# One load per attention tile, issued behind its buffer's last reader, and a third first-layer group queued ahead of step 0

## The chip, the cores and the metric

One core of a Trainium2 chip runs the kernel. The metric is the device time of one execution in microseconds (us), shown as the median of three runs. The engines are named as in the profile: PE (TensorE), PEld (its weight loads), DVE (VectorE), ACT (ScalarE), POOL (GpSimd) and SP (SyncE, which only issues DMAs).

## What is computed

The reference chains three parts over 3072 tokens (4 batches of 768) of width 384 (8 heads of 48):

```python
for t in range(S):                       # linear attention with decay w and bonus u
    cur = np.einsum('bhd,bhe->bhde', u[None] * kt, vt)
    y[:, :, t] = np.einsum('bhd,bhde->bhe', rt, state + cur)
    state = wt[..., None] * state + np.einsum('bhd,bhe->bhde', kt, vt)
h = x @ w_in                             # dense layer, 384 -> 2048 -> 384
x = (np.maximum(h, 0) + alpha * np.minimum(h, 0)) @ w_out
logits = xn @ en.T / tau                 # 8 experts, top 1 by cosine
out[mask] = gate_w[mask, None] * (np.maximum(x[mask] @ w1[e], 0) @ w2[e])
```

## The kernel before, in words

The tokens are cut into 24 tiles of 128 (tile n) and 8 blocks of three tiles (block j). The attention is done chunk by chunk, a tile at a time. Its work is split into ten pieces a0 to a9 (`ATT`, L393): a0 and a1 are decay scans on DVE (L261, L270), a2 and a3 transposes and scores on PE, a4 (`att_p4`) the outputs on PE (L362, L365), a5 the transposition of the result for the dense layer, a8 (`att_w`, L274) a check of the decays on ACT.

A tile's inputs come as one DMA of 1.35 MB on SP's queue (`load_att`, L157, issued at L165; two DMAs for tiles 0 to 5). The pool `ld` has two buffers, so the load of tile n+2 overwrites tile n (tile 2 has a place of its own) and waits for every reader of tile n, of which a4 is the last. `run` (L860) calls `load_att(n + 2)` behind each of the pieces 4, 8 and 9 of a tile n above 2. In the main loop pieces 4 and 8 occur, piece 9 doesn't.

The dense layer runs in steps T (loop at L950), 16 to a block. A step runs one group of the first layer (`l1`, 9 matmuls into `h_ps`, L407; ACT L411 and DVE L412 make `m`, ACT L421 and DVE L426 split it into `gh` and `gl`) and, two steps behind, one of the second layer (`l2`, 9 matmuls into three `o_ps`, L436). In the program's text a step is: split of block 0's `m`, pieces a2 to a5, l1, l2, pieces a0, a1, a6 and a8, and then `step`, which advances the routing. Pieces lie on steps by a table: tile n begins at step t0, piece a8 stands at t0+3, a4 at t0+6, and for a block j of 3 or more the three tiles have t0 = 16(j-1) + {-4, 1, 7} (`AT`, L81).

At the end of block j's second layer, at T = 16j+17, `o_evac` (L440) copies the three `o_ps` into `rows` (ACT L446, DVE L444). There are three `o_ps` buffers and one `rows` buffer. The routing (`route`, L452) works on `rows` a piece a step and stores its three parts to DRAM (`x2d`, L520, on SP's queue) at T = 16j+29, 16j+30 and 16j+31. The next `o_evac`, at T = 16j+33, needs these stores to be done.

Ahead of step 0 a list (`PLAN`, L78) orders the first attention pieces ("a2.1" is piece 2 of tile 1), the conversion of the dense weights ("c2.1": stage 2 of chunk 1; four stages L196, L198/L199, L210, L212 on ACT and DVE), the first groups of layer 1 ("l1.0") and matmuls that only keep PE busy ("w4": four of L391, which write the same two `ps_h` buffers as `h_ps`). The weights come in 16 chunks through four `stg` buffers (L185, L187, on SP's queue); a chunk's load is issued when the chunk four before it has been converted, in steps 0 to 10 two steps ahead of its use. In steps 32 to 55 SP also stores 24 tiles of zeros to `out` (L982), one a step. Later, experts are gathered and run (L689 to L796); the change doesn't touch that.

Of the kernel before, what the change touches and what calls it, by code (L numbers as in the profile page):

```python
# [22 lines left out]
NTILE = B * NCH  # L23
# [51 lines left out]
LAGS = [0, 1, 4, 4, 6, 7, 2]  # L75

LOADS = [(0, "w"), (0, "rk"), "id", "v", (0, "n"), "e", (1, "w"), (1, "rk"), (1, "n"), (2, "w"), (2, "rk"), (2, "n"), 0, 1, 2, 3, "u"]
PLAN = "a0.0 a1.0 a8.0 a2.0 w6 a6.0 a3.0 a7.0 w8 a0.1 a1.1 a6.1 s a4.0 a3.1 a9.0 a2.1 e c0.0 a7.1 a9.1 w8 a0.2 c0.1 c0.2 a1.2 a6.2 c1.0 a4.1 w8 a3.2 c1.1 a7.2 a5.0 a5.1 c2.0 w4 a4.2 p0.0 c3.0 a5.2 c2.1 c1.2 l1.0 c3.1 c2.2 l1.1 p1.0 c0.3 c3.2 w4 a8.1 a2.2 a9.2"  # L78

AT1 = [0, 4, 8]  # L80
AT = {2: [-1, 6], 3: [-4, 1, 7]}  # L81
# [12 lines left out]
def tile_main(ctx, tc, keep, x2d, tbl, att, w_in, w_out, alpha, u_row, u_col, emb, tau, w1, w2, cst, out):  # L94
# [62 lines left out]
    def load_att(n, part=None):  # L157
        if n not in ld_t:
            if n == 2:
                ld_t[n] = att2[:, 0:LD]  # L160
            else:
                ld_t[n] = ldp.tile([128, LD], F32, tag="ld", name="ld")
        m = LN + 2 * DM if n in ND else LN
        for s in {None: [slice(0, LN), slice(m, LD)] if n in ND else [slice(0, LD)], "w": [slice(LD - LW, LD)], "rk": [slice(0, LN)], "n": [slice(m, LD - LW)]}[part]:
            SP.dma_start(out=ld_t[n][:, s], in_=att[n][:, s])  # L165
# [15 lines left out]
    def load_stage(kind, g):  # L181
        t = sgp.tile([128, GF * DM, 2], I32, tag="sg", name="stg")
        if kind == "in":
            for k in range(KD):
                SP.dma_start(out=t[:, k * GF * 128:(k + 1) * GF * 128, :], in_=w_in[:, k, 2 * g * GF * 128:2 * (g + 1) * GF * 128])  # L185
        else:
            SP.dma_start(out=t, in_=w_out[:, g * GF:(g + 1) * GF, :])  # L187
        stage[kind, g] = t

    def conv(q, kind, g):  # L190

        t = stage[kind, g]
        lw, hw = t[:, :, 0], t[:, :, 1]
        lf = lw.bitcast(F32)
        if q == 0:
            ACT.activation(out=lf, in_=lw.bitcast(U32), func=AF.Copy, scale=-0.936 * 2.0 ** -51, bias=-2.0)  # L196
        elif q == 1:
            DVE.scalar_tensor_tensor(out=lw, in0=hw, scalar=3, in1=lw, op0=ALU.logical_shift_left, op1=ALU.bitwise_or)  # L198
            DVE.scalar_tensor_tensor(out=lw, in0=hw, scalar=0x3FFFFFFF, in1=lw, op0=ALU.bitwise_or, op1=ALU.bitwise_and)  # L199
        else:  # L200
            h, g0 = divmod(g, NG // 2)
            if kind == "in":
                hi, lo = (w[:, :, g0 * GW:(g0 + 1) * GW] for w in win[h])
            else:
                if h == len(wout):
                    wout_half()
                hi, lo = (w[:, g0 * GF:(g0 + 1) * GF, 0:DM] for w in wout[h])
            f3 = lf.rearrange("p (a b) -> p a b", a=(KD if kind == "in" else GF))
            if q == 2:
                ACT.activation(out=hi, in_=f3, func=AF.Copy, scale=-1.0)  # L210
            else:
                DVE.scalar_tensor_tensor(out=lo, in0=f3, scalar=-1.0, in1=hi.bitcast(F32), op0=ALU.mult, op1=ALU.subtract)  # L212
                del stage[kind, g]
# [173 lines left out]
    def warm(n):  # L387

        for _ in range(n):
            t = ps_h.tile([128, 3, 128], F32, tag="h", name="idle")  # L390
            PE.matmul(out=t, lhsT=oneb, rhs=oneb.rearrange("p (o t) -> p o t", o=1).to_broadcast([128, 3, 128]), start=True, stop=True)  # L391
# [4 lines left out]
    g_t, m_t, o_t = {}, {}, {}  # L396
# [20 lines left out]
    def l1_hi(j, f):  # L417
        nt = BLK[j] * CH
        gh = gp.tile([128, nt], F32R, tag="gh", name="gh")
        gl = gp.tile([128, nt], F32R, tag="gl", name="gl")  # L420
        ACT.activation(out=gh, in_=m_t[j, f], func=AF.Copy)  # L421
        g_t[j, f] = (gh, gl)

    def l1_lo(j, f):
        gh, gl = g_t[j, f]
        DVE.tensor_tensor(out=gl, in0=m_t.pop((j, f)), in1=gh.bitcast(F32), op=ALU.subtract)  # L426
# [376 lines left out]
    if True:  # L803
# [54 lines left out]
        ran = set()  # L858

        def run(kind, *a):  # L860
            if (kind, *a) in ran:
                return
            if kind != "w":
                ran.add((kind, *a))
            if kind == "a":
                q, n = a
                ATT[q](n)
                m = n + 3 if n < 2 else n + 2
                if q in (4, 8, 9) and n != 2 and m < NTILE and (n > 2 or {("a", i, n) for i in (4, 8, 9)} <= ran):
                    load_att(m)  # L870
            elif kind == "c":
                q, c = a
                conv(q, ("in", "out")[c % 2], c // 2)
                if q == 3 and c + NSG < 2 * NG:
                    load_stage(("in", "out")[(c + NSG) % 2], (c + NSG) // 2)
            elif kind == "w":
                warm(*a)
            elif kind == "l":
                (l1, l2)[a[0] - 1](0, a[1])
            elif kind == "p":  # L880
                (wprime_a, wprime_b)[a[0]](a[1])
            elif kind == "e":
                ep = ps_a.tile([128, KD, NE], F32, tag="a", name="ep")
                for k in range(KD):
                    PE.transpose(ep[:, k, :], en[:, k * 128:(k + 1) * 128], ident[0:NE, 0:NE])
                ACT.activation(out=enT, in_=ep, func=AF.Copy)
            else:
                DVE.tensor_scalar(out=en2, in0=en2, scalar1=1e-6, scalar2=None, op0=ALU.add)
                DVE.reciprocal(out=en2, in_=en2)
                ACT.activation(out=en, in_=en, func=AF.Copy, scale=en2)  # L890

        def pieces(T, qs):
            for q, n in sched.get(T, []):
                if q in qs:
                    run("a", q, n)
                    if q == 6:
                        run("a", 7, n)

        def convs(T, late):
            for q, i in CONV[late]:  # L900
                c = T + OFF - i
                if 0 <= c < 2 * NG:
                    run("c", q, c)
# [20 lines left out]
        def early_loads():  # L924
            for s in range(ES):
                ids_load(s)
                if s == 0:
                    pump()
                    yield
            for s in range(ES):  # L930
                for t in range(2):
                    gather(s, t)
                yield
# [13 lines left out]

        for t in PLAN.split():
            run(t[0], *(int(i) for i in t[1:].split(".") if i))
        for T in range(16 * NB + 2):  # L950
            j, f = divmod(T, 16)
            for k in sorted(k for k in m_t if k[0] == 0 and k[1] <= T):
                l1_hi(*k)
                l1_lo(*k)
            pieces(T, (2, 3, 4, 5))
            convs(T, 0)
            if j < NB:
                run('l', 1, f) if j == 0 else l1(j, f)
            for i, d in enumerate(WPD):
                c = T + OFF - d  # L960
                if c % 2 and 0 <= c < 2 * NG:
                    run("p", i, c // 2)
            if T == 16 * (NB - 1):
                xg.extend(atp.tile([128, 2, ROW], F32, tag=t, name="xg") for t in ("st", "st", "at"))
                for t in xg:
                    POOL.memset(t, 0.0)
            if T >= 2:
                run('l', 2, T - 2) if T < 18 else l2((T - 2) // 16, (T - 2) % 16)
                if (T - 2) % 16 == 15:
                    o_evac((T - 2) // 16)  # L970
                    q = (T - 2) // 16
                    bg.append(chain(route(q), *((early_table(), early_loads()) if q == NB - 2 else (last_table(),) if q == NB - 1 else ())))
            convs(T, 1)
            pieces(T, (0, 1, 6, 8))
            if j and (j, f) in m_t:
                l1_lo(j, f)
            step(STEP7 if j >= NB - 1 else 1)
            if T == 32:
                zero = sgp.tile([128, DM], F32, tag="sg", name="zero")
                POOL.memset(zero, 0.0)  # L980
            if 32 <= T < 32 + NTILE:
                SP.dma_start(out=out[(T - 32) * CH:(T - 31) * CH, :], in_=zero)  # L982
            for fn, i, at in EARLY:
                if T - 16 * NB == at:
                    (split, x_T)[fn](0, i)
# [31 lines left out]
        n = len(STEPS)  # L1017
# [318 lines left out]
```

## Time and profile before

| | us |
|---|---|
| median of 3 runs (lowest, highest) | 885.43 (881.11, 886.57) |
| the profiled execution | 884.76 |
| its span in the trace | 882.9 |
| PE busy, share of the span | 811.0, 92% |
| DVE, ACT, POOL busy | 582.1, 433.2, 299.7 |

The span is the traced part of the profiled execution; the execution's own time lies 1.9 us above it. A duration below is from that execution. "Idle before" of a row is the time in which its engine waited ahead of it, and the name behind it is what ended the wait. PEclk is the TensorE clock that was granted, 1.00 for 2.4 GHz and 0.50 for 1.2 GHz.

### The profile page before, as it was taken

What the parts mean: (1) busy time and instruction counts of PE and PEld (TensorE: products, weight loads), DVE (VectorE), ACT (ScalarE), POOL (GpSimd) and SP (SyncE); (2) the same over time, 40 slices, a digit from 0 to 9 for tenths busy, and PEclk for the clock granted to TensorE, in tenths of its full rate; (3) what the DMA queues carried; (4) which work ended last, traced back from release to release, by engine and by line L of the source; (5) the groups of instructions that cost most, each with busy time, mean ns of one, the idle gap of its engine ahead of it and who ended that gap; (6) DMA issues with size and microseconds to landing.
All of it is one profiled execution on the core that took longest, in us unless ns stands there. A gap on an engine that the chain in (4) does not pass through costs nothing. (4 is left out here: it accounts for less than half of the span.)

```text
span 882.9 us, 16507 instructions
## 1 busy us (share of the span) xinstructions
PE 811.0 (92%) x6466; PEld 768.6 (87%) x6466; DVE 582.1 (66%) x1229; ACT 433.2 (49%) x861; POOL 299.7 (34%) x365
## 2 busy tenths in 40 slices
PE   9798899995996999699799879999899999999996
PEld 5598799895996899699699879999789999999996
DVE  7798867764671676468358367372897776767672
ACT  6776544442342434234333343432555676767672
POOL 2012122241232222123212321214446777676641
PEclk9999999996999799799889989999999999999999
DMA  9636532456349255333503630006567778686850
GB/s 318 203 109 234 198 127 69 184 100 216 103 164 193 88 162 144 135 127 75 204 12 124 161 111 1 28 28 233 170 126 253 228 263 281 212 285 208 289 179 31
DMA packets 34504, 140.71 MB, mean 159 GB/s; under 512 B 6076, under 2 KB 13468, under 8 KB 29808
## 3 DMA queue, kind: packets, MB, share of 16 engines
q1 hardware_dynamic: 20464, 79.70, 29.1%
q0 software_dynamic: 13952, 59.86, 20.8%
q8 instruction: 53, 0.87, 0.4%
q14 instruction: 35, 0.29, 0.1%
HBM read 125.20 MB, written 15.51 MB: 159 GB/s over the span
## 5 line engine op out<-in xcount | busy, mean ns | idle before, releaser
L412 DVE TENSOR_TENSOR m<-h_ps,m 128x384 f32<-128x384 f32 x128 | 71.0, 554 | 110.5 <-ACT m L411 110.0
L411 ACT ACTIVATE m<-h_ps,al_sb 128x384 f32<-128x384 f32 x128 | 74.0, 578 | 141.2 <-PE h_ps L407 132.9
L421 ACT ACTIVATE gh<-m 128x384 fp32r<-128x384 f32 x128 | 67.2, 525 | 119.7 <-DVE m L412 118.4
L335 POOL TENSOR_SCALAR_AFFINE_SELECT A<-A 128x512 f32<-128x512 f32 x48 | 33.6, 723 | 209.7 <-ACT A L334 209.7
L426 DVE TENSOR_TENSOR gl<-m,gh 128x384 fp32r<-128x384 f32 x128 | 79.4, 621 | 37.8 <-ACT gh L421 36.5
L436 PE MATMUL o_ps<-wout0h,gh 128*128 128x392 f32 x192 | 71.7, 374 | 35.1 <-ACT rows L446 35.1
L689 POOL DMA_INDIRECT raw<-in_w,wix x64 | 66.5, 1040 | 51.0 <-DVE w0l L701 22.2
L731 PE MATMUL h_ps<-yh,w0h 128*128 128x256 f32 x264 | 77.5, 293 | 3.9 <-DVE g2l L736 3.8
L731 PE MATMUL h_ps<-yl,w0h 128*128 128x256 f32 x264 | 75.1, 284 | 0.9 <-DVE yl L722 0.9
L731 PE MATMUL h_ps<-yh,w0l 128*128 128x256 f32 x264 | 74.6, 283 | 0.0
L407 PE MATMUL h_ps<-xh,win0h 128*128 128x384 f32 x192 | 71.6, 373 | 2.3 <-DVE m L412 1.5
L701 DVE TENSOR_TENSOR w1l<-raw,w1h 128x768 fp32r<-128x768 f32 x64 | 60.8, 956 | 18.8 <-ACT w1h L700 15.2
L436 PEld LDWEIGHTS o_ps<-wout0h,gh 128*128 128x128 f32 x192 | 39.4, 205 | 36.8 <-ACT rows L446 36.7
L407 PE MATMUL h_ps<-xh,win1h 128*128 128x384 f32 x192 | 68.1, 355 | 1.6 <-DVE m L412 1.6
L436 PE MATMUL o_ps<-wout0l,gh 128*128 128x392 f32 x192 | 69.3, 361 | 0.0
L436 PE MATMUL o_ps<-wout0h,gl 128*128 128x392 f32 x192 | 69.1, 360 | 0.0
L701 DVE TENSOR_TENSOR w0l<-raw,w0h 128x768 fp32r<-128x768 f32 x64 | 60.6, 956 | 12.1 <-ACT w0h L700 11.5
L407 PE MATMUL h_ps<-xl,win0h 128*128 128x384 f32 x192 | 67.7, 352 | 0.1
L407 PE MATMUL h_ps<-xh,win0l 128*128 128x384 f32 x192 | 67.3, 351 | 0.0
L436 PE MATMUL o_ps<-wout1h,gh 128*128 128x392 f32 x192 | 65.8, 343 | 0.1
L436 PE MATMUL o_ps<-wout1h,gl 128*128 128x392 f32 x192 | 65.5, 341 | 0.0
L436 PE MATMUL o_ps<-wout1l,gh 128*128 128x392 f32 x192 | 65.3, 340 | 0.0
(282 smaller groups left out, 2301.4 us busy)
## 6 DMA issues: line engine op xcount, KB each, us to landing
ld<-in_att SPq DMA_DIRECT2D x36, 1348.5 KB, 6.4
stg<-in_w_in SPq DMA_DIRECT2D x24, 256.0 KB, 4.5
stg<-in_w_out SPq DMA_DIRECT2D x8, 768.0 KB, 7.8
x2d<-rows SPq DMA_DIRECT2D x24, 194.0 KB, 6.3
out<-zero SPq DMA_DIRECT2D x24, 192.0 KB, 6.9
ld<-in_att SPq DMA_DIRECT2D x6, 512.0 KB, 3.8
ld<-in_att SPq DMA_DIRECT2D x4, 452.5 KB, 8.0
raw<-in_w,wix POOLq DMA_INDIRECT x64
```

What stands on the lines that cost most here:

```text
L335: POOL.affine_select(out=h, in_=h, pattern=[[0, HP], [1, CH]], compare_op=ALU.is_gt, fill=0.0, base=0, channel_multiplier=-1)
L407: PE.matmul(out=h, lhsT=w[:, k, :], rhs=x[:, k, :], start=(n == 0), stop=(n == 3 * KD - 1))
L411: ACT.activation(out=m, in_=h, func=AF.Copy, scale=al_sb[:, f:f + 1])
L412: DVE.tensor_tensor(out=m, in0=h, in1=m, op=ALU.min)
L421: ACT.activation(out=gh, in_=m_t[j, f], func=AF.Copy)
L426: DVE.tensor_tensor(out=gl, in0=m_t.pop((j, f)), in1=gh.bitcast(F32), op=ALU.subtract)
L436: PE.matmul(out=o_t[j][i], lhsT=g[:, s], rhs=w, start=(f == 0 and n == 0), stop=(f == KF - 1 and n == 2))
L689: POOL.indirect_dma_start(out=t, out_offset=None, in_=src, in_offset=idx(wix[:, h, COL[s]:COL[s] + 1]))
L701: DVE.tensor_tensor(out=lo, in0=a, in1=hi.bitcast(F32), op=ALU.subtract)
L731: PE.matmul(out=h, lhsT=w[:, k, :], rhs=x[:, k, :], start=(n == 0), stop=(n == 3 * KD - 1))
```

## The change

`run` issues the load of tile n+2 once, behind a4 of tile n (for tiles 0 and 1, whose loads were issued once already, the rule stays). `PLAN` gets "g l1.2" ahead of its last four entries: "g" splits the `m` that are there, and l1.2 is the third group of block 0's first layer, which stood in step 2. The split is made a function, `flush`, which takes every `m` there is.

```diff
-PLAN = "... l1.1 p1.0 c0.3 c3.2 w4 a8.1 a2.2 a9.2"
+PLAN = "... l1.1 p1.0 c0.3 c3.2 g l1.2 w4 a8.1 a2.2 a9.2"
...
                 m = n + 3 if n < 2 else n + 2
-                if q in (4, 8, 9) and n != 2 and m < NTILE and (n > 2 or {("a", i, n) for i in (4, 8, 9)} <= ran):
+                if n != 2 and m < NTILE and (q == 4 if n > 2 else q in (4, 8, 9) and {("a", i, n) for i in (4, 8, 9)} <= ran):
                     load_att(m)
...
+            elif kind == "g":
+                flush()
...
+        def flush():
+            for k in sorted(k for k in m_t if k[0] == 0):
+                l1_hi(*k)
+                l1_lo(*k)
...
-            for k in sorted(k for k in m_t if k[0] == 0 and k[1] <= T):
-                l1_hi(*k)
-                l1_lo(*k)
+            flush()
```

SP's queue in the fourth block of the main loop, before. `ld` with a number is one tile's buffer, "x2" two issues in a row for the same tile, `x2d<-rows` a store of the routing.

```order
L165 DMA ld_4162<-in_att 128x2697 x2
L165 DMA ld_4426<-in_att 128x2697 x2
L520 DMA x2d_60<-rows_4003 128x388 x2
L165 DMA ld_4665<-in_att 128x2697
L520 DMA x2d_60<-rows_4003 128x388
L165 DMA ld_4665<-in_att 128x2697
L165 DMA ld_4903<-in_att 128x2697 x2
L165 DMA ld_5167<-in_att 128x2697 x2
```

The same place after the change:

```order
L165 DMA ld_4268<-in_att 128x2697
L165 DMA ld_4545<-in_att 128x2697
L520 DMA x2d_60<-rows_3988 128x388 x3
L165 DMA ld_4778<-in_att 128x2697
L165 DMA ld_5006<-in_att 128x2697
L165 DMA ld_5266<-in_att 128x2697
```

Every second issue of a load is gone, and the third store now stands ahead of the next tile's load.

SP's queue in steps 1 to 9, before: `stg` is a chunk of the dense weights, `ld_825` tile 5 and `ld_1123` tile 6.

```order
L165 DMA ld_825<-in_att 128x1024
L165 DMA ld_825<-in_att 128x905
L185 DMA stg_908<-in_w_in 128x512 x3
L187 DMA stg_958<-in_w_out 128x1536
L165 DMA ld_825<-in_att 128x1024
L165 DMA ld_825<-in_att 128x905
L185 DMA stg_1053<-in_w_in 128x512 x3
L187 DMA stg_1120<-in_w_out 128x1536
L165 DMA ld_1123<-in_att 128x2697
L185 DMA stg_1205<-in_w_in 128x512 x3
L187 DMA stg_1255<-in_w_out 128x1536
```

And after:

```order
L185 DMA stg_905<-in_w_in 128x512 x3
L187 DMA stg_955<-in_w_out 128x1536
L165 DMA ld_992<-in_att 128x1024
L165 DMA ld_992<-in_att 128x905
L185 DMA stg_1051<-in_w_in 128x512 x3
L187 DMA stg_1118<-in_w_out 128x1536
L185 DMA stg_1201<-in_w_in 128x512 x3
L187 DMA stg_1251<-in_w_out 128x1536
L165 DMA ld_1296<-in_att 128x2697
```

The loads of tiles 5 and 6 have moved behind the two chunks that stood behind them.

DVE around the end of `PLAN`, before (L426 is the split of an `m`, L198 the next chunk's conversion):

```order
L412 TENSOR_TENSOR m_606<-h_ps_596,m_606 128x384
L212 SCALAR_TENSOR_TENSOR win0l_131<-stg_169,win0h_130 128x3x256
L426 TENSOR_TENSOR gl_674<-m_589,gh_673 128x384
L198 SCALAR_TENSOR_TENSOR stg_173<-stg_173 128x768
L199 SCALAR_TENSOR_TENSOR stg_173<-stg_173 128x768
```

And after:

```order
L212 SCALAR_TENSOR_TENSOR win0l_131<-stg_169,win0h_130 128x3x256
L426 TENSOR_TENSOR gl_645<-m_589,gh_644 128x384
L426 TENSOR_TENSOR gl_649<-m_606,gh_648 128x384
L412 TENSOR_TENSOR m_662<-h_ps_652,m_662 128x384
L426 TENSOR_TENSOR gl_695<-m_662,gh_694 128x384
L198 SCALAR_TENSOR_TENSOR stg_173<-stg_173 128x768
```

Three instructions of later steps (the split of group 1, and both for group 2) now stand ahead of the chunk's conversion.

## Rows read from the trace of the kernel before

**Rows 1.** The page, part 1: busy us, share of the span, instructions.

```profile
PE 811.0 (92%) x6466; PEld 768.6 (87%) x6466; DVE 582.1 (66%) x1229; ACT 433.2 (49%) x861; POOL 299.7 (34%) x365
```

**Rows 2.** Waits of PE, 160 to 560 us: sum, times, longest.

```profile
PE o_ps L436 <- ACT rows L446: 35.1, 5, 8.8
```

**Rows 3.** Waits of ACT, 160 to 560 us.

```profile
ACT rows L446 <- DMA x2d<-rows: 50.3, 5, 11.9
```

**Rows 4.** Timeline of SP's queue, blocks 3 and 4: start, us, what.

```profile
334.92 6.35 SPq L165 DMA_DIRECT2D ld<-in_att  x2
...
355.18 0.34 SPq L165 DMA_DIRECT2D ld<-in_att  x1
355.57 0.42 SPq L520 DMA_DIRECT2D x2d<-rows  x1
```

**Rows 5.** Waits of SP's queue, whole span.

```profile
SPq L165 <- PE y_ps L365: 267.9, 18, 24.8
```

**Rows 6.** DMA issues: count, KB each, median us to landing.

```profile
ld<-in_att SPq DMA_DIRECT2D x36, 1348.5 KB, 6.4
...
stg<-in_w_out SPq DMA_DIRECT2D x8, 768.0 KB, 7.8
x2d<-rows SPq DMA_DIRECT2D x24, 194.0 KB, 6.3
```

**Rows 7.** PE in the 10 us behind each of the five waits: busy, PEclk, DMA.

```profile
210.78:220.78 10.00, 8.91 (x34) 0.62 0.50 169
...
287.51:297.51 10.00, 8.92 (x29) 0.53 0.52 172
...
362.66:372.66 10.00, 8.89 (x30) 0.54 0.31 123
...
437.61:447.61 10.00, 8.91 (x29) 0.53 0.31 125
...
511.94:521.94 10.00, 9.67 (x46) 0.83 0.33 129
```

**Rows 8.** Timeline of PE while the clock comes back behind the second wait.

```profile
296.12 0.53 PE L436 MATMUL o_ps<-wout0h,gl 128*128 128x392 f32 x1
296.45 0.52 PE L436 MATMUL o_ps<-wout0h,gh 128*128 128x392 f32 x1
...
297.33 0.34 PE L436 MATMUL o_ps<-wout0l,gh 128*128 128x392 f32 x1
297.51 0.34 PE L436 MATMUL o_ps<-wout0h,gl 128*128 128x392 f32 x1
```

**Rows 9.** Line L520, the routing's stores, all 24.

```profile
DMA to landing us min/median/max: 2.3/6.3/14.5
```

**Rows 10.** Timeline of steps 5 to 11: start, us, what, [idle before].

```profile
65.51 0.80 SPq L165 DMA_DIRECT2D ld<-in_att  x2
...
66.42 1.37 SPq L185 DMA_DIRECT2D stg<-in_w_in  x3
...
73.10 0.88 ACT L196 ACTIVATE stg<-stg 128x768 f32<-128x768 uint32 x1 [3.70 <-DMA stg<-in_w_in]
...
74.71 1.46 PE L232 MATMUL wt_ps<-ident,stg 128*128 128x128 f32 x6 [2.24 <-ACT s_wp L247]
...
100.58 0.99 PE L232 MATMUL wt_ps<-ident,stg 128*128 128x128 f32 x6 [2.07 <-ACT s_wp L247]
```

**Rows 11.** All engines behind the first of these waits: PE, PEld, DVE, ACT, POOL busy, PEclk, DMA.

```profile
74.70:79.00 4.30, 4.29 (x17) 4.06 (x18) 4.30 (x7) 4.06 (x10) 2.27 (x3) 0.60 0.76 250
```

**Rows 12.** Timeline around the end of the written order.

```profile
35.64 1.00 DVE L212 SCALAR_TENSOR_TENSOR win0l<-stg,win0h 128x768 fp32r<-128x768 f32 x1
...
36.06 0.60 PE L321 MATMUL kt_ps<-ident,att 128*128 128x128 f32 x4
...
39.42 0.56 DVE L426 TENSOR_TENSOR gl<-m,gh 128x384 fp32r<-128x384 f32 x1 [2.78 <-ACT gh L421]
39.89 0.95 DVE L198 SCALAR_TENSOR_TENSOR stg<-stg 128x768 int32<-128x768 int32 x1
```

More of the change, by code (lines that the diff above doesn't have):

```diff
@@ L77 @@
 LOADS = [(0, "w"), (0, "rk"), "id", "v", (0, "n"), "e", (1, "w"), (1, "rk"), (1, "n"), (2, "w"), (2, "rk"), (2, "n"), 0, 1, 2, 3, "u"]
-PLAN = "a0.0 a1.0 a8.0 a2.0 w6 a6.0 a3.0 a7.0 w8 a0.1 a1.1 a6.1 s a4.0 a3.1 a9.0 a2.1 e c0.0 a7.1 a9.1 w8 a0.2 c0.1 c0.2 a1.2 a6.2 c1.0 a4.1 w8 a3.2 c1.1 a7.2 a5.0 a5.1 c2.0 w4 a4.2 p0.0 c3.0 a5.2 c2.1 c1.2 l1.0 c3.1 c2.2 l1.1 p1.0 c0.3 c3.2 w4 a8.1 a2.2 a9.2"
+PLAN = "a0.0 a1.0 a8.0 a2.0 w6 a6.0 a3.0 a7.0 w8 a0.1 a1.1 a6.1 s a4.0 a3.1 a9.0 a2.1 e c0.0 a7.1 a9.1 w8 a0.2 c0.1 c0.2 a1.2 a6.2 c1.0 a4.1 w8 a3.2 c1.1 a7.2 a5.0 a5.1 c2.0 w4 a4.2 p0.0 c3.0 a5.2 c2.1 c1.2 l1.0 c3.1 c2.2 l1.1 p1.0 c0.3 c3.2 g l1.2 w4 a8.1 a2.2 a9.2"
 AT1 = [0, 4, 8]
```

## The prediction

> **What bounds the kernel now.** I read the busy times first. PE is busy 92% of the span, the next engine 66% [rows 1], so PE's order is the path, and what counts is where PE stands still or runs slowly. The table of PE's waits in the main loop comes next. One wait holds nearly all of it: five times the second layer's first matmul waits for `o_ps`, which ACT has not yet copied into `rows`, 35.1 us in all [rows 2]. ACT in turn waited, the same five times, for a store `x2d<-rows` of the routing to land, because `rows` has one buffer [rows 3]. So the question is why the store is late, and SP's queue answers it [rows 4]: at 355.18 a tile's load goes out, and 0.4 us behind it, at 355.57, the store. The load had been waiting for PE's last read of the tile in that buffer, as 18 loads did, 24.8 us at the longest [rows 5], and SP's queue is served in order, so the store waited with it. In the written order the load stands there because piece a8 asks for it at T = 16j+31, ahead of the third store of the same step, while its buffer comes free only with a4 at T = 16j+34, one step after `o_evac` needs the store (T = 16j+33). The wait is built into the order and comes once per block, for j = 0 to 4, which is five times. The same rows show the second flaw: 36 loads of 1.35 MB for 18 tiles [rows 6], each issued again 6 us after the first (two in 6.35 us [rows 4]).
>
> **The change part by part.** *The third store.* After the change nothing that waits for a later a4 stands ahead of a store. The load ahead of the three stores is the one that a4 releases at T = 16j+29 or 30, three or four steps before `o_evac`; in block 3 that is the one at 334.92 [rows 4]. The stores then go out at about 335 to 337 instead of up to 355.57. PE restarts at 362.66 [rows 7] after some 7 us of waiting (35.1 over 5), so it ran dry near 355.7, 19 us after the new issue. A store takes 6.3 us in the median and 14.5 at most [rows 9]. Both fit, so I take the whole wait as gone: 35.1 us.
>
> What comes with it is the clock. In the five stretches of 10 us behind the waits PEclk is 0.62, 0.53, 0.54, 0.53 and 0.83 [rows 7]; with two levels, 0.50 and 1.00, that is 7.6 + 9.4 + 9.2 + 9.4 + 3.4 = 39.0 us at the lower one. PE was idle for 4.7 us of these 50 (1.09 + 1.08 + 1.11 + 1.09 + 0.33), which leaves 34.3 us of slow work. A matmul of the second layer starts every 0.33 us there and every 0.18 us afterwards [rows 8], so 46% of it is lost: 15.8 us. The 4.7 us of idle are the attention's result coming late because DVE stood in its own copy of `o_ps`; I count them too. Together 35.1 + 15.8 + 4.7 = 55.6 us. If only the idle times came back, it would be 39.8.
>
> The rows thus price the lower clock at 15.8 us. The Trainium skill (TensorE: Matmul & The Clock Gate, Terms) prices it as the throttled time times one minus the ratio, here half: 39.0 us would be 19.5, and the sum 59.3. The difference is that the rule also prices the throttled time in which PE had nothing to do, and these rows show 4.7 us of it, and a loss per matmul of 46% and not 50%.
>
> What is late next? Between the waits PE has no other wait of size (DVE and ACT are far less busy), so a block becomes bound by PE's own work at the full clock. The loads move the other way: one load now goes out when the first went out before, since that one had waited for the same a4, and its tile is complete 6 us earlier than with the second copy. On SP's queue the stores and the zero stores to `out` gain, nothing is moved behind a longer wait.
>
> *The weight chunks in steps 5 to 11.* At 65.51 the load of tile 5 goes out, released by a4 of tile 3, and a chunk of weights right behind it at 66.42; ACT stands 3.70 us for this chunk, and PE 2.24 [rows 10]. In the 4.3 us behind it PEclk is 0.60 [rows 11], 3.4 us slow, 1.6 lost. The pattern comes once more at tile 6, with 2.07 us on PE [rows 10]. After the change both chunks stand ahead of the tile's load and go out when their buffer has been converted, some 4.7 us sooner. Gross gain 2.24 + 1.6 + 2.07 = 5.9 us. But the next chunk is late then: it is issued two steps (about 8 us) ahead of its use, and `w_out` chunks land 7.8 us after their issue [rows 6], so I give 1 us back at each place. Net 3.9, bounded by 0 (the next chunk takes all of it) and 5.9.
>
> *Group l1.2 ahead of step 0.* It needs L212, which ends at 36.64 [rows 12]; its nine matmuls then end near 38.2, ACT's L411 and DVE's L412 near 39.5. The four filler matmuls behind it share the two `ps_h` buffers and wait for that L412. So the transposes of a2.2 start near 40.1 and not at 36.06. From there to the end of the split L426 the row chain takes 3.92 us (36.06 to 39.98), and L198, queued behind the split of group 2 now, starts at about 44.0 and not at 39.89 [rows 12]: 4.1 us later, of which three split and minimum instructions of about 0.56 us (1.7) are work brought forward. DVE loses 2.4 us. PE gains nine matmuls and waits longer ahead of the chunk's transposes, at a lower clock again. I take a cost of 3 us, between a gain of 2 (the nine matmuls, with the slip absorbed) and a loss of 6 (the slip plus another stretch at the low clock).
>
> *Sum.* 55.6 + 3.9 - 3.0 = 56.5 us. From the profiled execution, 884.76, that leaves 828.3. It lies 0.7 us under the median of the runs, so a median of 829.
>
> **The rivals.** *Part of the wait stays.* Each store now stands directly behind a load of 1.35 MB, and a load and a store side by side take 6.3 to 14.5 us. In steps 32 to 55 zero stores stand among them. For the wait to come back a third store would have to land 19 us after the load's release; the longest of 24 took 14.5 [rows 9]. If half of it stays, the gain is 27.8 + 0.9, the time 857. On the ring the Trainium skill (DMA: Bandwidth & Descriptors, Queues, rings and completion order) speaks against the new order, since descriptors of one queue are consumed in ring order on each DMA engine: a store behind a load cannot move its bytes first. The trace agrees, with a minimum of 2.3 us and a median of 6.3, near the 6.4 of a load.
>
> *It doesn't do what it says.* The releaser in [rows 3] is inferred; if `rows` were held by another reader of the routing, the stores' new place would be worth nothing and only the start changes: 884, within 1%. Against it: the store of 355.57 [rows 4] with a median landing of 6.3 us [rows 9] is there at 361.9, and PE restarted at 362.66 [rows 7].
>
> *Slower: the single load comes too late.* Before, the load was asked for at a8. If it now went out so late that a0 of tile n+2 waited for it, DVE's scans would stop and PE behind them, for 18 tiles. From a4 of tile n to a0 of tile n+2 there are 4 to 5 steps of about 4 us, 16 to 20 us, against 6.4 us for a load [rows 6]. It decides from 16 us upwards. At 21 us per load each tile would cost 5 us, 90 in all less the 56.5: 918. What speaks against it is that the first copy never went out earlier than a4 [rows 5].
>
> **How the numbers follow.** The forecast gets 0.87, the half wait 0.08, no effect 0.03, the late load 0.02. The likeliest case alone runs from 820 (no cost at the start, the chunks' whole 5.9, a further us or two) to 846 (39.8 us of idle time, no clock, and the start at its worst). For 8 in 10 I take 817 to 847; the half wait at 857 lies outside. Faster by over 1% are the first two cases, 0.95; within 1%, 0.03; slower, 0.02. About 1% is what a measurement of this kernel tells from no change.
>
> **What would show it.** Right: L165's full-size loads count 18 and not 36; PE's wait for `rows` is gone from its table or under 5 us in sum; the three stores of a block go out together some 19 us ahead of `o_evac`; PEclk stays at 1.00 from 160 to 560 us; PE's restarts at 362.66 and 437.61 [rows 7], 74.95 us apart with one wait and its aftermath between them, come about 64 us apart (74.95 less a fifth of 55.6). For the start: ACT's waits for chunks of 3.70 us and more shrink to 1 or 2 us, and L198 at the end of the written order starts near 44 us. Wrong: the wait for `rows` stands with the stores issued early (then they land late), or DVE's L261 waits for `ld`.

## The result and the profile after

The changed kernel takes 819.84 us in the median of 4 runs, against 883.46 for 4 runs of the kernel before on the same chip: a ratio of 0.9276, with a 95% interval of 0.9239 to 0.9314, that is 63.6 us less. The prediction was 829 us, with a range of 817 to 847, so the direction and the size came out, and the gain is some 9 us larger than the likeliest case. The profiled execution took 818.76 us with a span of 816.9, 66.0 us shorter than the span before. One run in all that follow, the third of `e1_loads_alone` (956.10 us at a granted clock of 0.75), was in a slow state; its ratio leaves it out, and its median of 816.66 would be 816.43 without it.

First come the busy times and the DMA issues on the page of the changed kernel, to be held against [rows 1] and [rows 6].

```profile
PE 793.8 (97%) x6466; PEld 755.7 (93%) x6466; DVE 582.0 (71%) x1229; ACT 435.2 (53%) x861; POOL 300.9 (37%) x365
...
HBM read 99.36 MB, written 15.51 MB: 141 GB/s over the span
...
ld<-in_att SPq DMA_DIRECT2D x18, 1348.5 KB, 5.8
...
x2d<-rows SPq DMA_DIRECT2D x24, 194.0 KB, 7.3
```

PE executes the same 6466 matmuls in 17.2 us less, so a part of the gain is not idle time but speed. The loads of a whole tile are 18 and no longer 36. The two landing times of a store, 7.3 us here and 6.3 before, say little: the profile holds a landing for 10 of the 24 stores here, and for only 6 of those of [rows 6] and [rows 9].

Next are the waits of PE, of SP's queue and of DVE from 160 to 560 us. [rows 2] has the same stretch; [rows 5] has the whole span, and its 267.9 us are 224.7 in this stretch.

```profile
PE h_ps L407 <- DVE m L412: 1.5, 1, 1.5
```

```profile
SPq L165 <- PE y_ps L365: 207.4, 14, 23.1
SPq L520 <- DVE rows L502: 78.5, 3, 38.6
```

```profile
DVE rows L444 <- DMA x2d<-rows: 0.6, 1, 0.6
```

The wait for the evacuated rows, 35.1 us before, is gone altogether, and one small wait of another kind is all that is left of PE's. SP's queue still stands 207.4 us for y_ps. That costs nothing now, although stores still stand behind such a load: the load is the one whose tile comes free early enough, as the next rows show. (SP's wait for the rows themselves is not new; it was 71.0 us in this stretch before.) Of DVE's waits for a store, 53.2 us in five before, 0.6 us is left, in the first of the blocks that had been late.

The timeline of SP's queue for the same blocks as [rows 4]:

```profile
305.21 0.34 SPq L165 DMA_DIRECT2D ld<-in_att  x1
305.65 3.13 SPq L520 DMA_DIRECT2D x2d<-rows  x3
325.48 44.15 SPq L165 DMA_DIRECT2D ld<-in_att  x3
369.73 1.57 SPq L520 DMA_DIRECT2D x2d<-rows  x3
```

The three stores of a block go out together, right behind the one load. From that load to the next evacuation (ACT's L446 at 323.37) there are 18.2 us. In the first of the five blocks that had been late it is only 15.1 (180.25 to 195.32), and there the 0.6 us are. These distances turn out to be the numbers by which most of the experiments below are decided.

Last, the span cut at the first and the seventh of the eight evacuations of `o_ps`, so that the middle holds six blocks; the evacuations that came late before are the second to the sixth. The columns are the stretch, its length, the busy times of PE, PEld, DVE, ACT and POOL, the granted clock, DMA. First the kernel before, then the changed one; PE and DVE run the same number of instructions in each stretch.

```profile
0.00:130.92 130.92, 116.48 (x1317) 100.45 (x1318) 105.12 (x157) 80.40 (x175) 24.62 (x48) 0.96 0.58 200
130.92:571.19 440.27, 399.04 (x3226) 382.52 (x3225) 265.47 (x631) 168.87 (x353) 105.93 (x145) 0.94 0.41 120
571.19:882.90 311.71, 295.49 (x1927) 285.59 (x1925) 211.50 (x444) 183.94 (x337) 169.12 (x172) 0.99 0.60 197
```

```profile
0.00:129.28 129.28, 118.48 (x1317) 101.44 (x1318) 104.12 (x157) 81.22 (x174) 24.26 (x48) 0.93 0.52 174
129.28:510.68 381.40, 381.34 (x3226) 368.76 (x3225) 266.58 (x631) 169.27 (x352) 107.49 (x145) 1.00 0.24 81
510.68:816.90 306.22, 294.00 (x1927) 285.46 (x1925) 211.31 (x444) 184.66 (x337) 169.14 (x172) 0.99 0.61 201
```

The six blocks in the middle give 58.9 of the 66.0 us. PE's idle time there falls from 41.2 us (440.27 less 399.04) to 0.06, and its busy time by 17.7 us, with the granted clock rising from 0.94 to 1.00. The start gives 1.6 us and the tail 5.5. The start is known to some 2 us only: a second profile of the changed kernel (`e11_after_again`) has its first evacuation at 127.21.

### The profile page after: what moved, and what is told of

Same layout as the page of the kernel before. It is cut to its first block, busy times and chain, and to the rows that moved or that the text cites. A ratio compares the mean times of both kernels' runs of the same rounds, so it can differ in the third digit from the quotient of the medians.

```text
span 816.9 us, 16480 instructions
## 1 busy us (share of the span) xinstructions
PE 793.8 (97%) x6466; PEld 755.7 (93%) x6466; DVE 582.0 (71%) x1229; ACT 435.2 (53%) x861; POOL 300.9 (37%) x365
## 2 busy tenths in 40 slices
DMA packets 31623, 114.86 MB, mean 141 GB/s; under 512 B 5756, under 2 KB 13148, under 8 KB 29232
## 3 DMA queue, kind: packets, MB, share of 16 engines
q1 hardware_dynamic: 17584, 53.85, 19.5%
HBM read 99.36 MB, written 15.51 MB: 141 GB/s over the span
## 5 line engine op out<-in xcount | busy, mean ns | idle before, releaser
L412 DVE TENSOR_TENSOR m<-h_ps,m 128x384 f32<-128x384 f32 x128 | 71.0, 555 | 97.3 <-ACT m L411 96.6
L426 DVE TENSOR_TENSOR gl<-m,gh 128x384 fp32r<-128x384 f32 x128 | 81.3, 636 | 38.2 <-ACT gh L421 38.0
L407 PE MATMUL h_ps<-xh,win0h 128*128 128x384 f32 x192 | 69.2, 360 | 2.3 <-DVE m L412 1.5
L436 PE MATMUL o_ps<-wout0h,gh 128*128 128x392 f32 x192 | 66.7, 347 | 0.0
L407 PE MATMUL h_ps<-xh,win0l 128*128 128x384 f32 x192 | 65.4, 341 | 1.1 <-DVE win0l L212 1.1
L436 PE MATMUL o_ps<-wout0l,gh 128*128 128x392 f32 x192 | 65.9, 343 | 0.0
L436 PE MATMUL o_ps<-wout0h,gl 128*128 128x392 f32 x192 | 65.9, 343 | 0.0
L407 PE MATMUL h_ps<-xl,win0h 128*128 128x384 f32 x192 | 65.5, 341 | 0.1
L407 PE MATMUL h_ps<-xh,win1l 128*128 128x384 f32 x192 | 64.9, 338 | 0.0
```

The lines of the kernel that those rows point to most:

```text
L407: PE.matmul(out=h, lhsT=w[:, k, :], rhs=x[:, k, :], start=(n == 0), stop=(n == 3 * KD - 1))
L412: DVE.tensor_tensor(out=m, in0=h, in1=m, op=ALU.min)
L436: PE.matmul(out=o_t[j][i], lhsT=g[:, s], rhs=w, start=(f == 0 and n == 0), stop=(f == KF - 1 and n == 2))
```

## The experiments

Two theories stand against each other here. By mine, time was lost because a load that waits for its tile's readers held up the store behind it on SP's queue (the place). By the rival, the surplus loads and their 25.8 MB (140.71 less 114.86) cost the time (the bytes). The change mends both at once.

**The two halves of the change by themselves.** `e1_loads_alone` has the changed loads and the old order at the start; `e2_plan_alone` has the new order and the old loads.

```diff
 e1_loads_alone, against the changed kernel
-... l1.1 p1.0 c0.3 c3.2 g l1.2 w4 a8.1 a2.2 a9.2"
+... l1.1 p1.0 c0.3 c3.2 w4 a8.1 a2.2 a9.2"
...
-            flush()
+            for k in sorted(k for k in m_t if k[0] == 0 and k[1] <= T):
+                l1_hi(*k)
+                l1_lo(*k)

 e2_plan_alone, against the changed kernel
-                if n != 2 and m < NTILE and (q == 4 if n > 2 else q in (4, 8, 9) and {("a", i, n) for i in (4, 8, 9)} <= ran):
+                if q in (4, 8, 9) and n != 2 and m < NTILE and (n > 2 or {("a", i, n) for i in (4, 8, 9)} <= ran):
```

> Only the loads are changed (each tile from the fifth on loaded once, behind a4); the order at the start is that of the kernel before. My theory (the third store of a block's rows was held up by the second and third load of the same tile; the early split of group 2 costs about 3 us): 816 to 818 us, 2 to 3 us under the changed kernel's 819.8, with evacuation of o L446 coming every 64 us and the first L198 of group 2 back near 39.9. Rival 1 (the early split is itself worth something): 821 us or more. Rival 2 (the gain needs both halves of the change): over 840 us.

> Only the order at the start is changed (group 2's matmuls and its split ahead of the first step's pieces); the loads are issued three times as before. My theory: 3 us slower than the kernel before, 881 to 889 us, with evacuations of o still 75 us apart and TensorE's wait for the evacuated rows still about 35 us between 160 and 560 us. Rival (the early group 2 brings a part of the gain): 875 us or less.

The loads alone measured 816.66 us (ratio 0.9263 [0.9216, 0.9310]), the order alone 886.86 (1.0057 [1.0034, 1.0080]), against 880.61 for the kernel before. So all of the gain is in the loads, and the new order costs some 5 us beside the old loads. In `e2_plan_alone` the wait of [rows 2] is there as before:

```profile
PE o_ps L436 <- ACT rows L446: 39.3, 5, 10.8
```

**Place or bytes.** `e4_once_at_a8` takes the bytes away and leaves the place; `e3_twice_behind_a4` has the right place and all of the surplus bytes.

```diff
 e4_once_at_a8
-... (q == 4 if n > 2 else ...
+... (q == 8 if n > 2 else ...

 e3_twice_behind_a4
-                    load_att(m)
+                    for _ in range(2 if n > 2 else 1):
+                        load_att(m)
```

> The changed kernel, with each tile from the fifth on loaded once, but issued behind a8, where the kernel before issued its second load. The surplus traffic is gone, the place on SP's queue is not that of the change. My theory: the load either stands on SP's queue ahead of a store until a4's readers are done, so that TensorE waits for the rows again (about 35 us between 160 and 560 us) and the time is 865 to 885 us. Rival (the traffic was what cost the time, the place does not matter): 819 to 825 us.

> The changed kernel, with each tile from the fifth on loaded twice, one load right behind the other, both issued behind a4. This keeps the position and brings back half of the surplus traffic (14 of the 28 surplus loads of 1.35 MB). My theory (what cost the time is that the later loads waited on SP's queue for the tile's last readers, ahead of the stores): 819 to 823 us, no wait of TensorE for the evacuated rows. Rival (the surplus bytes themselves cost the time): half of the 64 us comes back, 845 us or more.

`e4_once_at_a8` measured 877.61 us (ratio 0.9958 [0.9935, 0.9982]). It moves 114.86 MB, as the changed kernel does, and gains 3 us. It has the new order at the start too, and against `e2_plan_alone`, which shares that, it gains 9 us. Its waits of PE, and SP's queue behind them:

```profile
PE o_ps L436 <- ACT rows L446: 29.8, 5, 6.8
```

```profile
352.20 0.34 SPq L165 DMA_DIRECT2D ld<-in_att  x1
352.58 1.03 SPq L520 DMA_DIRECT2D x2d<-rows  x1
```

The expectation of `e3_twice_behind_a4` has a miscount: the written order runs two of the three pieces that ask for a load in the main loop, so each tile was loaded twice before [rows 6] and not three times, and this kernel moves the same 140.71 MB as the kernel before, not half of the surplus.

The two rows of `e4_once_at_a8` are the picture of [rows 4] again, with a single load: the third store goes out 0.4 us behind a load that had to wait. From the first to the seventh evacuation it takes 432.5 us, where the kernel before takes 440.3 and the changed one 381.4: the bytes alone give 7.8 of 58.9 us there, and as the whole of the cause that rival falls. But `e3_twice_behind_a4` missed my figure: 848.62 us (0.9619 [0.9578, 0.9660]), 29 us over the changed kernel and inside what the rival had said, though with all of the bytes back and not half. Its waits of PE, its SP queue, and the landing times of its stores:

```profile
PE o_ps L436 <- DVE rows L444: 17.8, 3, 9.1
PE t_ps L381 <- DVE y L367: 6.7, 6, 1.6
```

```profile
320.36 7.87 SPq L165 DMA_DIRECT2D ld<-in_att  x2
328.34 1.82 SPq L520 DMA_DIRECT2D x2d<-rows  x3
```

```profile
DMA to landing us min/median/max: 1.9/11.9/20.5
```

The second load waits for the first to land, so the stores go out 8.0 us behind the load and not 0.4 us; and they land after up to 20.5 us, since the second load's bytes are ahead of them. In the block shown the last of the three lands 18.3 us after its issue, some 27 us after the load, which is far more than the 18.2 us there are. ACT waits for a store in all five blocks, 29.6 us in sum. Either part could be at fault, or both.

**The wait without the bytes, and the bytes without the wait.** `e8_wait_without_bytes` makes the second load tiny; `e9_bytes_without_wait` sends the bytes elsewhere.

```diff
 e8_wait_without_bytes
                     load_att(m)
+                    if n > 2:
+                        SP.dma_start(out=ld_t[m][0:1, 0:128], in_=att[m][0:1, 0:128])

 e9_bytes_without_wait
                     load_att(m)
+                    if n > 2:
+                        SP.dma_start(out=dup.tile([128, LD], F32, tag=f"dup{m}", name="dup"), in_=att[m])
```

> The changed kernel, and behind each load of a tile from the fifth on a second load of only 512 bytes into the same tile: it waits on SP's queue until the first has landed, as the second load did in e3_twice_behind_a4, but moves next to nothing. Theory 1 (what cost 29 us in e3 was that the queue stood still for the 6 us of the first landing, with stores behind it): 840 to 849 us. Theory 2 (it was the second load's bytes, ahead of the stores): 819 to 824 us. If both are needed because each alone fits into the slack of some 7 to 10 us that the stores have in the changed kernel: 819 to 826 us here and in e9_bytes_without_wait.

> The changed kernel, and behind each load of a tile from the fifth on a copy of the same 1.35 MB from the input into scratch memory in HBM: the bytes of the second load are read again ahead of the stores, but SP's queue waits for nothing (the copy is written to HBM, not to SBUF). Theory 1 (the wait on the queue cost the 29 us in e3_twice_behind_a4): 819 to 826 us. Theory 2 (the bytes ahead of the stores did): 840 us or more, with TensorE waiting for the evacuated rows again. If it takes both: 819 to 826 us.

`e8_wait_without_bytes` measured 819.65 us (0.9297 [0.9244, 0.9350]), the same as the changed kernel, although SP's queue stands still for the landings:

```profile
SPq L872 <- DMA ld<-in_att: 83.5, 15, 7.1
```

```profile
303.98 0.33 SPq L165 DMA_DIRECT2D ld<-in_att  x1
309.60 0.25 SPq L872 DMA_DIRECT2D ld<-in_att  x1
309.95 1.32 SPq L520 DMA_DIRECT2D x2d<-rows  x3
```

The stores go out 6.0 us behind the load, and PE waits for none of them (DVE for one, 0.5 us; the profile holds no landing of a store in this run). `e9_bytes_without_wait` measured 836.64 us (0.9508 [0.9439, 0.9576]), 17 us over the changed kernel and between my figures for it. In the profiled execution, at 831.52 us the fastest of its four, PE waits for the rows 5.8 us in two blocks of the five, and ACT for the stores:

```profile
202.46 0.89 ACT L447 ACTIVATE rows<-o_ps 128x392 f32<-128x392 f32 x2 [7.80 <-DMA x2d<-rows]
270.31 0.89 ACT L447 ACTIVATE rows<-o_ps 128x392 f32<-128x392 f32 x2 [3.85 <-DMA x2d<-rows]
```

```profile
DMA to landing us min/median/max: 1.9/7.4/15.5
```

These are the first two of the five. In the first, ACT was ready at 194.66 (202.46 less 7.80), 15.1 us behind the load at 179.59, and was held for 22.9. In the second, zero stores to `out` stand between the three stores, and it was held for 22.1 us behind the load at 248.20, where 18.3 would have done. In the other three the stores go out 2.1 to 3.6 us behind the load (315.72, and 317.82 with 1.48 us for three), the three landings of theirs that the profile holds (8 of the 24 in all) took 12.3 to 14.2 us, and ACT waits for none. (These copies are read from HBM and written to HBM again, 41.75 MB written and not 15.51, so they move more than a second load does, and 17 us may be too much for its bytes.) My simple theory falls with this, and a budget takes its place: from the release of the load to the evacuation there are 15.1 us in the first block and about 18 in the others, and the store's delay on the queue and its landing must fit in together. The wait alone fits in all five blocks, the bytes alone in three, both together in none.

**The stores off SP's queue, the bytes kept.** `e7_stores_by_act` is the kernel before with one edit: ScalarE issues the stores.

```diff
-            SP.dma_start(out=x2d[t0:t0 + CH, :], in_=rows[:, i, 0:ROW])
+            ACT.dma_start(out=x2d[t0:t0 + CH, :], in_=rows[:, i, 0:ROW])
```

> The kernel before with all its surplus loads, and one edit: the stores of a block's rows (L520) are issued by ScalarE and so stand on its queue, no longer behind the loads on SP's. My theory (time was lost because a load that waits for its tile's readers holds up the store behind it): TensorE's wait for the evacuated rows goes, evacuations of o come 64 to 66 us apart, and the time is 820 to 832 us (the early waits for weight chunks stay, and ScalarE pays for 24 issues). Rival (the surplus 26 MB cost the time on the DMA engines, whichever queue the stores are on): 845 us or more.

It measured 849.78 us (0.9607 [0.9528, 0.9685]): half of the gain, inside what the rival had said and 18 us above my figure. ACT's timeline in block 3, then the landing times of the stores:

```profile
331.17 0.34 ACTq L520 DMA_DIRECT2D x2d<-rows  x1
...
334.69 0.34 ACTq L520 DMA_DIRECT2D x2d<-rows  x1
...
337.88 0.34 ACTq L520 DMA_DIRECT2D x2d<-rows  x1
...
352.04 0.89 ACT L446 ACTIVATE rows<-o_ps 128x392 f32<-128x392 f32 x2 [5.56 <-DMA x2d<-rows]
```

```profile
DMA to landing us min/median/max: 2.0/8.2/16.8
```

The third store goes out at 337.88 and not at 355.57 [rows 4], unblocked, and still ACT is held until 352.04 by its landing, 14.0 us later. But this is not the place that the change gives it. ACT issues the stores in the order of its own instructions, one in each step, and the third goes out 8.6 us ahead of the time at which ACT is ready to write `rows` again (352.04 less 5.56); in the changed kernel all three are out 14.6 us ahead of it (308.78 and 323.37), and a landing of 14.0 us would have fitted. SP issues the surplus second load at 336.41, 1.5 us ahead of the store, and the DMA engines are busy throughout in the 6 us that follow (1.14 is the next to last column, their share over all queues):

```profile
337.00:343.00 6.00, 6.00 (x46) 5.67 (x45) 1.68 (x3) 3.85 (x9) 2.25 (x4) 1.00 1.14 114
```

So the run shows that 32 us come from taking the stores out from behind the waiting loads (881.76 less 849.78). It does not show how much of the rest is the surplus bytes and how much the later issue.

From the first to the seventh evacuation, which leaves the start out, the kernel before takes 440.3 us, `e4_once_at_a8` (bytes mended) 432.5, `e3_twice_behind_a4` (place mended, both loads kept) 411.8, `e7_stores_by_act` 411.5 and the changed kernel 381.4. The bytes alone give 7.8 us, the place alone 28.5, and both together 58.9, more than the two added. In the kernel before each of the two flaws thus covered a part of what the other cost.

**The weight chunks.** `e5_tiles56_as_before` issues the loads of tiles 5 and 6 as before (twice each, by the profile, where its expectation says three times).

```diff
-... (q == 4 if n > 2 else ...
+... (q in (4, 8, 9) if 2 < n < 5 else q == 4 if n > 4 else ...
```

> The changed kernel, but the loads of tiles 5 and 6 are issued three times each, as in the kernel before; later tiles once. My prediction's term for the weight chunks of steps 5 to 11: ScalarE's waits of 3.70 us and more for the chunks near 73 us and after come back, and the time is 3.9 us over the changed kernel's 819.8 (823 to 826 us), with block intervals of 64 us kept. Rival (the chunk term is nothing, the gain at the start came from elsewhere): 818 to 821 us.

It measured 826.40 us (0.9375 [0.9315, 0.9435]). ACT's two waits for chunks are back, 4.38 and 5.20 us, and PE's two behind them:

```profile
78.44 0.99 PE L232 MATMUL wt_ps<-ident,stg 128*128 128x128 f32 x6 [2.51 <-ACT s_wp L247]
...
104.03 1.18 PE L232 MATMUL wt_ps<-ident,stg 128*128 128x128 f32 x6 [1.81 <-ACT s_wp L247]
```

The first evacuation comes at 134.39 and not at 129.28, 5.1 us later (7.2 against the second profile of the changed kernel), and from there to the seventh it takes 381.3 us, as the changed kernel does. By the medians the term is 6.6 us; the interval of this ratio and that of the changed kernel just do not touch (0.9315 and 0.9314).

**The order at the start.** Four kernels ran side by side on one chip, five times each.

```diff
 e6_split_later, against the changed kernel
-            flush()
+            for k in sorted(k for k in m_t if k[0] == 0 and k[1] <= T):
+                l1_hi(*k)
+                l1_lo(*k)

 e10_splits_alone, against e1_loads_alone
-... p1.0 c0.3 c3.2 w4 a8.1 a2.2 a9.2"
+... p1.0 c0.3 c3.2 g w4 a8.1 a2.2 a9.2"
...
+            elif kind == "g":
+                for k in sorted(k for k in m_t if k[0] == 0):
+                    l1_hi(*k)
+                    l1_lo(*k)
```

> The changed kernel again, on the same chip and beside the same runs of the kernel before as the three runs that follow, for differences of a few us: 819 to 821 us.

> The kernel of e1_loads_alone again (the changed loads with the old order at the start). My theory (the early group 2 costs about 3 us): 2 to 4 us under e11_after_again. Rival (the difference of 3.2 us seen so far was between chips): within 1 us of it.

> The changed kernel, but the split of group 2 (ScalarE's L421 and VectorE's L426) is put back to step 2, behind the first step's conversion of a weight chunk; its matmuls and the splits of groups 0 and 1 stay early. My theory (the 3 us are VectorE's 3.08 us wait in the L426 of group 2, ahead of the conversion at L198): L198 starts near 40 to 41 instead of 44 us, and the time is within 1 us of e12_loads_alone_again. Rival (TensorE's earlier matmuls of group 2 cost the time): within 1 us of e11_after_again.

> The kernel of e1_loads_alone with one edit: the split of group 1 is put directly behind that of group 0, ahead of the first step (what the mark g does without the l1.2 behind it). My theory: no cost of its own, since both groups are ready by then: within 1 us of e12_loads_alone_again, perhaps 1 us under it. Rival (the early splits, not group 2's, cost the 3 us): within 1 us of e11_after_again.

| kernel | median us | ratio to before, 95% | L198 starts, us |
|---|---|---|---|
| e11_after_again | 820.38 | 0.9283 [0.9256, 0.9310] | 43.33 |
| e12_loads_alone_again | 817.07 | 0.9248 [0.9221, 0.9275] | 41.20 |
| e6_split_later | 816.31 | 0.9239 [0.9212, 0.9266] | 40.68 |
| e10_splits_alone | 814.10 | 0.9219 [0.9193, 0.9246] | 39.05 |

Here L198 is the first conversion behind the written order (39.89 before [rows 12]). The order of the times is the order in which it starts. Its start alone is no safe measure, for two profiles of the same kernel have it 1.5 us apart (39.69 in `e1_loads_alone`, 41.20 in `e12_loads_alone_again`). But counted from the start of the conversion ahead of it (DVE's L212 on `win0l`) it is 4.26 us in both, and in the order of the table 7.32, 4.26, 3.68 and 2.09. What holds it up is the split of group 2 on VectorE, first in `e11_after_again` and then in `e10_splits_alone`:

```profile
42.86 0.56 DVE L426 TENSOR_TENSOR gl<-m,gh 128x384 fp32r<-128x384 f32 x1 [3.08 <-ACT gh L421]
43.33 0.95 DVE L198 SCALAR_TENSOR_TENSOR stg<-stg 128x768 int32<-128x768 int32 x1
```

```profile
38.11 1.03 DVE L426 TENSOR_TENSOR gl<-m,gh 128x384 fp32r<-128x384 f32 x2
39.05 0.95 DVE L198 SCALAR_TENSOR_TENSOR stg<-stg 128x768 int32<-128x768 int32 x1
```

Putting only that split back wins the 4 us (`e6_split_later`; its interval overlaps that of the changed kernel by a thousandth). The early matmuls of group 2 are all that `e6_split_later` has beyond `e10_splits_alone`: L198 comes 1.6 us later with them, since group 2's L412 stands ahead of it, and the time is 2.2 us longer by the medians, though the intervals overlap. In `e10_splits_alone` the splits of groups 0 and 1 stand together and wait for nothing, where group 0's alone waited 2.78 us before [rows 12]. I had expected 1 us of that at most, and it is 3.0 by the medians, though that step alone is not beyond the intervals. Against the changed kernel it is: `e10_splits_alone` is the fastest version found, below both kernels, 6.3 us under the changed one.

## Why the prediction was right, and where it was off

**The third store.** The table of windows gives 41.2 us of idle time in the six blocks. That is what the prediction had, 35.1 and 4.7, and 1.4 us more in PE's waits ahead of the transposes, which it left out. The place where it looked was the right one: with the old place and fewer bytes little is gained (`e4_once_at_a8`). But the step that gave the whole 35.1 to the store's place was too simple. It called the doubled loads the second flaw and gave them no term of their own beside the store, on the ground that 14.5 us of landing fit into 19. `e3_twice_behind_a4` shows that with nothing ahead of the stores that waits for a later a4, but with the loads doubled, the stores still land too late in all five blocks. The forecast holds because the change does both. Nor was the ground a firm one: [rows 9] holds a landing for 6 of the 24 stores, and `e2_plan_alone`, with the same loads, for 22, with 17.1 us at most. The limit of 19 us behind the load's release is 18.2 by the changed kernel's own profile, and 15.1 in the first block. There the changed kernel just fits: in `e11_after_again` the last store of that block lands at 192.7, 14.5 us behind the load and 0.4 us ahead of the evacuation. The forecast counted on 4.5 us to spare (19 less 14.5); that 0.4 sufficed is in part luck.

**The clock.** Between the first and the seventh evacuation PE's busy time fell by 17.7 us, against 15.8 worked out from the five windows of 10 us and 19.5 by the rule of the Trainium skill (TensorE: Matmul & The Clock Gate, Terms). Over the whole stretch the granted clock is 0.94 of 440.27 us, which with the two levels of 1.2 and 2.4 GHz is some 53 us at the lower one; half of that, as the rule has it, would be 26 us. The rule thus prices too high here, because the clock had already fallen within the waits, when PE had nothing to run. These are the 35.1 us of the five waits, with PE's busy time first and PEclk next to the DMA columns:

```profile
201.95:210.78 8.83, 0.01 (x1) 0.00 (x0) 0.54 (x2) 0.55 (x2) 1.98 (x2) 0.65 0.81 229
279.29:287.51 8.22, 0.00 (x1) 0.00 (x1) 0.55 (x2) 0.55 (x2) 0.00 (x0) 0.74 0.82 255
356.83:362.66 5.83, 0.00 (x0) 0.00 (x0) 0.52 (x2) 0.55 (x2) 0.00 (x0) 0.92 0.79 275
431.96:437.61 5.65, 0.01 (x1) 0.01 (x1) 0.54 (x2) 0.56 (x2) 0.00 (x0) 0.92 0.79 278
505.37:511.94 6.57, 0.00 (x1) 0.01 (x1) 0.54 (x2) 0.56 (x2) 0.00 (x0) 0.73 0.68 231
```

Worked out as in the prediction, they hold some 16 us at the lower level. With the 39.0 of the five windows behind them that is about all of the 53, so the 1.9 us that those windows miss do not come from a slow stretch elsewhere; where they come from stays open.

**The start.** The prediction had the chunks at a net 3.9 us, gross 5.9; they measured 5.1 and 7.2 against the two profiles of the changed kernel, and 6.6 by the medians. The 1 us that it gave back at each place was not lost, for ACT's longest wait for a later chunk is 0.3 us in the changed kernel. Group l1.2 was put at a cost of 3.0 us, and L198 at about 44.0 us. It started at 44.17, and the cost is 3.2 and 3.3 us in the two comparisons of the loads alone with the changed kernel. In sum 1.6 us were gained at the start in the one profile, 3.7 in the other, against the 0.9 predicted.

**The tail** was put at nothing, and the profile shows 5.5 us. Most of that is no effect of the change: `e2_plan_alone` has the loads of before, and its tail from the seventh evacuation is 308.0 us, 3.7 us shorter than that of the profiled execution before, 311.71. The tails of the other kernels are 306 to 308. What is left, up to 1.8 us, is within the spread of one profile.

In sum: 58.9 in the blocks where 55.6 stood, 1.6 for 0.9, and 5.5 for 0 make 66.0 for 56.5 in the two profiled executions. Of the 9.5 us between them 1.9 are the clock's, 1.4 the waits left out and 3.7 the odd tail of the one profile; the remaining 2.5 are spread over the rest of the tail and the start.

**The rivals.** That the change would do nothing, and that the single load would come too late, are both wrong: no wait of DVE's L261 for a tile's load is left over 2.1 us, and that one is at the start. Half of the wait staying is not what the changed kernel shows, but 17 us more in `e9_bytes_without_wait`, and the 0.6 us of DVE's wait in the first block, say that it was not far away. That a store does not pass a load on the ring is not shown by the 2.3 and 6.3 us that the prediction names for it; it is shown by pairs such as the load at 264.35 and the store at 264.79 before, which land after 12.1 and 12.4 us, at 276.5 and 277.2.

**The range.** Its ends do not follow from the terms beside them. Idle time alone, with nothing from the chunks and the start at its loss of 6, is 884.8 - 39.8 + 6.0 = 851.0, not 846; the low end is 884.8 - 55.6 - 5.9 = 823.3, or 821 with two more, not 820. The measured time lies below both low ends, because the blocks and the tail gave more than their terms.

## What to carry to other kernels

A DMA that waits for its buffer stops every DMA behind it on the same issuing queue; put its issue behind the last reader of that buffer, or its successors pay for its wait. Before pricing a late store, write down its budget, from what releases it to who needs it, and add the delay on the queue and the landing time behind whatever else is moving: a delay that fits alone and bytes that nearly do can miss it together, and mending one of two flaws shows less than its share. And instructions brought forward on an engine that serves in order are free only if their inputs are ready.

## What was not expected of the hardware

A store on a queue of its own does not land sooner. On ACT's queue, beside SP's doubled loads, the stores landed after 8.2 us in the median and 16.8 at most (`e7_stores_by_act`); on SP's queue, among the same loads, after 8.8 and 17.1 (`e2_plan_alone`; 22 of the 24 landings are in either profile). The Trainium skill says so (DMA: Bandwidth & Descriptors, Issuing engines are not separate DMA queues), and adds that issuing from several engines saves only the issue time. The first half agrees with these rows. The second does not: with the same loads and the same bytes, the other queue took 32 us off the kernel before, since a store there no longer stands behind a load that waits.

A queue that stands still for 83.5 us in 15 waits costs nothing (`e8_wait_without_bytes`), and taking 25.8 MB of 140.71 off the DMA engines gained 7.8 us in the blocks as long as the stores stood in the wrong place (`e4_once_at_a8`). With the stores behind a4's load, doubling the loads costs 30.4 us there (`e3_twice_behind_a4` against the changed kernel). What a wait or a saved byte is worth depends on whether the store behind it still makes its time.
